# An instruction order that is computed without a port shared by VectorE and GpSimd

## The chip, the core and the metric

The kernel runs on one core of a Trainium2 chip. Five engines of that core work side by side, each with its own queue that it takes in order: PE (TensorE, matmuls), DVE (VectorE), ACT (ScalarE), POOL (GpSimd) and SP (SyncE, which only issues transfers here). They wait for each other through semaphores. The metric is the device time of one execution in microseconds; before the change it was 1264.18 us, the median of three runs (1261.29 to 1264.84).

## The reference

Three layers follow one another: an attention without a square score matrix (softmax of q over the head's width, softmax of k over the sequence, then two products), a two-matrix layer with a quadratic gate, and four experts with ReLU that are weighted by normalised probabilities.

```
q_s = softmax(q, axis=-1);  k_s = softmax(k, axis=2)      # q, k, v: 4 x 8 x 576 x 64
x   = q_s @ (k_s^T @ v)                                   # laid out as 2304 tokens x 512
h   = x @ w_in                                            # w_in 512 x 2048, float64
g   = where(h >= 1, h, where(h <= -1, 0, (h + 1)^2 / 4))
y   = g @ w_out                                           # w_out 2048 x 512, float64
p   = probs / (sum(probs) + 1e-9)
out = sum over e of p[:, e] * (max(y @ w1[e], 0) @ w2[e]) # 4 experts, 512 x 1024 x 512
```

All outputs are float32, and the matmuls keep that precision by splitting each operand into a rounded high part and a low part (the rest).

## The kernel before

**Matmuls in triples.** A product of two operands is three matmuls: low x high, high x low, high x high (lines 912, 913 and 914). One such triple for 512 columns is the unit of PE's work. Most of PE's instructions are these. Each operand has to be split first: a cast to the high part (ACT or DVE, line 387 or 389) and a subtraction that leaves the low part (line 392, on DVE or on POOL; `combine` chooses the engine).

**Tiles and stages.** The 2304 tokens are five blocks (512, 512, 512, 256, 512). Blocks 0 and 1 make the first pass; blocks 2, 4 and 3 the second. In each pass the gated layer comes first ("a"), 16 chunks of 128 of its width, and then the four experts ("b"). For the experts, and in the second pass for the gated layer too, two blocks of tokens are multiplied together by a scheme of Strassen's kind: seven products instead of eight, for which sums and differences of the operands are formed. `prepare` (not quoted) does that for the tokens: T1 to T4 are differences, and seven operands (B11, T2, B21, T3, T1, T4, B22) are split, each in two halves. These steps read two operands from SBUF, and run when a block's last sums arrive, that is at the passage from "a" to "b": at about 240 to 272 us in the first pass and 815 to 850 us in the second.

**The head.** The attention of batches 0 and 1 (eight units of two heads) runs at the start, while the first weights arrive. The weights of the gated layer are float64. DVE and ACT turn each half of a chunk from its two 32-bit words into a high and a low part (`split_double`, lines 623, 627, 629, 631, 635, 642, 646: six instructions on DVE; the low part is done with line 646). The two parts are also written back to memory for the second pass (line 656, `kept`). Attention steps on DVE are the maximum of k (737, 742), of q (831), sums (850), reciprocals (852, 853, 805, 808) and the low part of x (889); POOL subtracts and scales q (line 392 on 640 columns).

**What sets the order.** Nothing is ordered by hand. `Order` holds a set of tasks (Python generators), each of which yields what it wants next: an engine with a duration, a choice of engines, a buffer, or an event. `Order.run` keeps a clock for each engine, takes the instruction that can start first (within 0.05 us the one with the smallest due time), gives it to its engine, and moves the clock. The instructions are issued in the sequence that comes out, so the computed clocks decide two things: the order within each engine's queue, SP's transfers included, and which engine gets a step that may run on either. On the chip, the queues then run as fast as their semaphores let them.

The durations are formulas by width (`dve`, `dve2`, `act`, `pool`, `pe`). DVE's work has two kinds. `dve` is an instruction that reads PSUM or is a reduction; `dve2` is one from SBUF to SBUF with two operands, or a fast copy. The table `HELD` says which clocks an instruction of each kind occupies.

Of the kernel before, what the change touches and what calls it, by code (L numbers as in the profile page):

```python
# [20 lines left out]
PE, ACT, DVE, POOL, SP = "PE", "ACT", "DVE", "POOL", "SP"  # L21


DVE2, PORT = "DVE2", "PORT"
HELD = {PE: (PE,), ACT: (ACT,), DVE: (DVE,), DVE2: (DVE, PORT), POOL: (POOL, PORT), SP: (SP,)}


class Event:
# [36 lines left out]
class Order:  # L65
# [63 lines left out]
    def run(self):  # L129
        while self.tasks:  # L130
            seq = None
            while seq != self.seq:
# [5 lines left out]
            assert ways, "no task can go on"  # L138
            start, e = min((w[0], HELD[w[1]][0]) for w in ways)
            _, start, _, e, d, t = min(  # L140
                (self.rank(w[3], e), w[0], w[3].seq, w[1], w[2], w[3])
                for w in ways if HELD[w[1]][0] == e and w[0] <= start + self.NEAR
            )
            self.now = max(self.now, start)
            for r in HELD[e]:
                self.clock[r] = start + d
            e = HELD[e][0]
            self.load[e] = (start, self.busy(e, start) + d)
# [11 lines left out]
    def way(self, t):  # L160
# [3 lines left out]
        for e, d in [t.want] if isinstance(t.want, tuple) else t.want:  # L164
            own = HELD[e][0]
            start = max(
                t.time - (self.HOP if own == t.engine else 0.0), *(self.clock[r] for r in HELD[e])
            )
# [1202 lines left out]
```

## Time and profile before

| | |
|---|---|
| median of three runs | 1264.18 us |
| the profiled execution | 1265.98 us |
| its span, first to last instruction | 1264.2 us |
| mean granted TensorE clock | 0.986 of full speed |
| PE busy | 1218.1 us (96%) |
| DVE busy | 709.7 us (56%) |
| ACT busy | 521.8 us (41%) |
| POOL busy | 572.4 us (45%) |

Matmuls overlap, so that a single one shows 0.39 us where one follows the other every 0.23 us. An engine's busy time counts the time in which at least one of its instructions runs. A DVE or POOL instruction that is held up after its start shows as a longer one, not as idle time.

### The profile page before, as it was taken

To read this page: it belongs to the slowest core of one execution; us is meant where nothing else is said; L and a number is where in the kernel's file an instruction comes from. 1 tells how busy PE (TensorE), PEld (TensorE's weight loads), DVE (VectorE), ACT (ScalarE), POOL (GpSimd) and SP (SyncE) were. 2 spreads that over 40 slices of the span, in tenths; PEclk is the share of its full clock that TensorE was granted. 3 is DMA by queue.
4 is the path that set the end of the run, shared out by engine and by line. 5 is a ranking of instruction groups with operands and counts; after the bars stand their busy time and mean duration, and the time that the engine had idled before them with its cause. 6 is when DMAs were issued, how large, how long until landed. Compare 5 with 4: busy or idle time off the path is not lost.

```text
span 1264.2 us, 15633 instructions
## 1 busy us (share of the span) xinstructions
PE 1218.1 (96%) x5692; PEld 1002.2 (79%) x5692; DVE 709.7 (56%) x1137; ACT 521.8 (41%) x986; POOL 572.4 (45%) x560
## 2 busy tenths in 40 slices
PE   6789999988999999999999999999999999999998
PEld 4468888767888788888878888878888888888886
DVE  5887989666655655435563555874344334343333
ACT  4477676633433433323565453633223132232320
POOL 2312222666645556543565746656243353432500
PEclk9889999989999999999999999999999999999999
DMA  7665665304323212111422221112111111211003
GB/s 195 169 186 186 199 182 172 111 18 125 96 65 109 76 47 85 34 65 37 135 82 100 84 102 49 51 34 67 34 61 39 34 34 34 67 34 34 17 1 84
DMA packets 86733, 105.39 MB, mean 83 GB/s; under 512 B 29056, under 2 KB 61824, under 8 KB 86656
## 3 DMA queue, kind: packets, MB, share of 16 engines
q1 hardware_dynamic: 86656, 104.40, 26.9%
q8 instruction: 45, 0.74, 0.2%
q14 instruction: 32, 0.26, 0.1%
HBM read 82.87 MB, written 21.50 MB: 83 GB/s over the span
## 4 chain that ended last, share of the span: by engine, by line
PE 84%; DVE 8%; ACT 3%; DMA 2%; issue 1%; SPq 1%; POOL 0%; DVEq 0%; ACTq 0%; POOLq 0%
PE bank L912 27%; PE bank L913 26%; PE bank L914 26%; PE bank L798 2%; PE bank L876 1%; DVE cv L631 1%; DVE cv L635 1%; PE bank L866 1%; DVE x L392 1%; DVE acc L392 1%; DVE cv L1228 1%; DVE cv L642 1%; DVE w L646 1%; DVE acc L1293 1%; DMA acc<-in_v_dram 1%
## 5 line engine op out<-in xcount | busy, mean ns | idle before, releaser
L912 PE MATMUL bank<-x,w 128*128 128x512 f32 (+1 forms) x880 | 329.3, 374 | 8.7 <-DVE w L646 5.4
L913 PE MATMUL bank<-x,w 128*128 128x512 f32 (+1 forms) x880 | 325.2, 370 | 6.2 <-DVE x L392 6.2
L914 PE MATMUL bank<-x,w 128*128 128x512 f32 (+1 forms) x880 | 324.0, 368 | 0.0
L392 POOL TENSOR_TENSOR w<-raw,w 128x512 fp32r<-128x512 f32 (+1 forms) x128 | 159.7, 1253 | 284.0 <-ACT w L387 277.8
L912 PEld LDWEIGHTS bank<-x,w 128*128 128x128 f32 x880 | 167.2, 190 | 43.2 <-DVE w L646 7.0
L913 PEld LDWEIGHTS bank<-x,w 128*128 128x128 f32 x880 | 167.4, 190 | 34.5 <-DVE x L392 8.2
L914 PEld LDWEIGHTS bank<-x,w 128*128 128x128 f32 x880 | 167.2, 190 | 27.5
L1309 DVE SCALAR_TENSOR_TENSOR acc<-bank,pn,acc 128x512 f32<-128x512 f32 x126 | 87.9, 748 | 125.0 <-PE bank L914 125.0
L387 ACT CAST w<-raw 128x512 fp32r<-128x512 f32 (+1 forms) x191 | 109.6, 600 | 73.1 <-PE bank L914 66.0
L912 PE MATMUL bank<-w,gate 128*128 128x512 f32 x342 | 138.7, 406 | 0.5 <-DVE gate L1204 0.5
L392 POOL TENSOR_TENSOR gate<-cv,gate 128x512 fp32r<-128x512 f32 (+1 forms) x54 | 68.6, 1271 | 147.0 <-ACT gate L387 132.0
L913 PE MATMUL bank<-w,gate 128*128 128x512 f32 x342 | 133.9, 392 | 0.0
L914 PE MATMUL bank<-w,gate 128*128 128x512 f32 x342 | 133.9, 392 | 0.0
L392 POOL TENSOR_TENSOR w<-cv,w 128x512 fp32r<-128x512 f32 x80 | 104.7, 1309 | 59.0 <-ACT w L387 48.7
L387 ACT CAST w<-cv 128x512 fp32r<-128x512 f32 x112 | 69.3, 619 | 118.9 <-POOL cv L392 95.1
L1202 ACT ACTIVATE gate<-bank 128x512 fp32r<-128x512 f32 (+1 forms) x73 | 40.5, 555 | 127.5 <-PE bank L914 73.8
L912 PE MATMUL bank<-w,gate_late 128*128 128x512 f32 x234 | 91.1, 390 | 0.0
L913 PE MATMUL bank<-w,gate_late 128*128 128x512 f32 x234 | 91.1, 389 | 0.0
L914 PE MATMUL bank<-w,gate_late 128*128 128x512 f32 x234 | 91.0, 389 | 0.0
L913 PE MATMUL bank<-gate,w 128*128 128x512 f32 (+1 forms) x216 | 81.3, 376 | 1.4 <-POOL gate L392 1.3
L912 PE MATMUL bank<-gate,w 128*128 128x512 f32 (+1 forms) x216 | 81.7, 378 | 0.7 <-ACT gate L387 0.6
L914 PE MATMUL bank<-gate,w 128*128 128x512 f32 (+1 forms) x216 | 81.0, 375 | 0.0
(154 smaller groups left out, 2003.2 us busy)
## 6 DMA issues: line engine op xcount, KB each, us to landing
raw<-in_moe_w_dram SPq DMA_DIRECT2D x64, 512.0 KB, 3.5
kept<-w SPq DMA_DIRECT2D x64, 256.0 KB, 3.8
raw<-kept SPq DMA_DIRECT2D x32, 512.0 KB, 3.3
raw<-in_moe_w_in_dram SPq DMA_DIRECT2D x16, 512.0 KB, 4.3
raw<-in_moe_w_out_dram SPq DMA_DIRECT2D x16, 512.0 KB, 4.2
out_dram<-acc SPq DMA_DIRECT2D x36, 128.0 KB, 2.4
wide<-in_k_dram SPq DMA_DIRECT2D x24, 160.0 KB, 3.1
wide<-in_v_dram SPq DMA_DIRECT2D x48, 80.0 KB, 2.6
```

The source lines that it names most:

```text
L387: nc.scalar.copy(out=dst, in_=src)
L392: (nc.vector if engine == DVE else nc.gpsimd).tensor_tensor(**kw)
L631: nc.vector.scalar_tensor_tensor(out=f, in0=low, scalar=2.0 ** -32, in1=ti, op0=ALU.mult, op1=ALU.add)
L635: nc.vector.scalar_tensor_tensor(out=mi, in0=top, scalar=-0x80000000, in1=mi, op0=ALU.bitwise_and, op1=ALU.bitwise_or)
L642: nc.vector.tensor_scalar(out=ti, in0=mi, scalar1=-0x800000, scalar2=None, op0=ALU.bitwise_and)
L646: nc.vector.scalar_tensor_tensor(out=lo, in0=f, scalar=2.0 ** -20, in1=t, op0=ALU.mult, op1=ALU.mult)
L798: nc.tensor.matmul(bank[:, :N], ek[:, c, :], vt_buf[:, c * N:(c + 1) * N], start=(c == 0), stop=(c == NC - 1),)
L912: nc.tensor.matmul(ps, al, bh, start=first, stop=False, **kw)
L913: nc.tensor.matmul(ps, ah, bl, start=False, stop=False, **kw)
L914: nc.tensor.matmul(ps, ah, bh, start=False, stop=last, **kw)
L1202: nc.scalar.activation(out=gh, in_=h, func=AF.Relu)
L1309: nc.vector.scalar_tensor_tensor(out=dst, in0=p, scalar=by, in1=dst, op0=ALU.mult, op1=ALU.add)
```

## The change

Before, an instruction of the kind `dve2` occupied DVE's clock and a clock named PORT, and a POOL instruction POOL's clock and PORT; so the computed order never lets the two run at the same computed time. Now each occupies its engine alone. Formulas, choices and tasks are unchanged.

```diff
 DVE2, PORT = "DVE2", "PORT"
-HELD = {PE: (PE,), ACT: (ACT,), DVE: (DVE,), DVE2: (DVE, PORT), POOL: (POOL, PORT), SP: (SP,)}
+HELD = {PE: (PE,), ACT: (ACT,), DVE: (DVE,), DVE2: (DVE,), POOL: (POOL,), SP: (SP,)}
```

The order differs on every engine. Three places are shown. In these rows a name is that of the written tile, then those it reads; numbers tell buffers apart (`w` weight parts, `raw` weights as loaded, `cv` temporaries, `x` operands of the matmuls, `acc` and `wide` buffers of attention and of sums).

The first is DVE's queue in the head. Before, from its 33rd instruction on:

```order
L889 TENSOR_TENSOR x_73<-bank_143,x_71 128x256
L642 TENSOR_SCALAR cv_124<-cv_123 128x512
L737 TENSOR_TENSOR wide_153<-wide_151 128x256
L889 TENSOR_TENSOR x_77<-bank_143,x_75 128x64
L889 TENSOR_TENSOR x_73<-bank_143,x_71 128x256
L805 TENSOR_SCALAR rk_168<-bank_142 128x2
L808 RECIPROCAL rk_168<-rk_168 128x2
L737 TENSOR_TENSOR mk_163<-wide_153 128x128
L737 TENSOR_TENSOR mk_163<-mk_163,wide_151 128x128
L646 SCALAR_TENSOR_TENSOR w_93<-cv_125,cv_124 128x512
```

The same place of DVE's queue now, from the 33rd instruction on:

```order
L642 TENSOR_SCALAR cv_124<-cv_123 128x512
L646 SCALAR_TENSOR_TENSOR w_93<-cv_125,cv_124 128x512
L629 TENSOR_SCALAR cv_127<-raw_121 128x512
L631 SCALAR_TENSOR_TENSOR cv_128<-raw_121,cv_127 128x512
L889 TENSOR_TENSOR x_73<-bank_144,x_71 128x256
L635 SCALAR_TENSOR_TENSOR cv_126<-raw_121,cv_126 128x512
L642 TENSOR_SCALAR cv_127<-cv_126 128x512
L646 SCALAR_TENSOR_TENSOR w_95<-cv_128,cv_127 128x512
L623 TENSOR_SCALAR cv_130<-raw_122 128x512
L889 TENSOR_TENSOR x_77<-bank_141,x_75 128x64
```

The first two conversions (w_93, w_95) have moved ahead of the keys of batch 1 (L737 on `wide`), of which there is none here yet; before, w_95 was the 69th instruction, and now it is the 40th.

The second is SP's queue in the head, where the key loads of batch 1 go to `wide`. Before:

```order
L787 DMA acc_88<-in_v_dram 64x5x64 x4
L689 DMA wide_151<-in_k_dram 64x2x320 x2
L478 DMA raw_120<-in_moe_w_out_dram 128x512
L787 DMA acc_90<-in_v_dram 64x5x64 x4
L689 DMA wide_154<-in_q_dram 64x2x320 x2
L689 DMA acc_91<-in_k_dram 64x2x320
L656 DMA kept_0_356<-w_92 128x512
L656 DMA kept_0_356<-w_93 128x512
```

And SP's queue now, from the same transfers on:

```order
L478 DMA raw_120<-in_moe_w_out_dram 128x512
L787 DMA acc_88<-in_v_dram 64x5x64 x3
L656 DMA kept_0_315<-w_92 128x512
L656 DMA kept_0_315<-w_93 128x512
L787 DMA acc_88<-in_v_dram 64x5x64
L787 DMA acc_90<-in_v_dram 64x5x64 x3
L656 DMA kept_1_343<-w_94 128x512
L656 DMA kept_1_343<-w_95 128x512
L787 DMA acc_90<-in_v_dram 64x5x64
L689 DMA wide_152<-in_k_dram 64x2x320 x2
```

The load of k for batch 1 has moved behind the writes of two converted halves, which wait for DVE's line 646.

The third is POOL's queue at the passage to the experts in the second pass (815 to 850 us). Before, from its 412th instruction on:

```order
L392 TENSOR_TENSOR cv_123<-acc_91,acc_89 128x512
L392 TENSOR_TENSOR cv_129<-acc_91,acc_89 128x512
L392 TENSOR_TENSOR w_119<-cv_125,w_115 128x512
L392 TENSOR_TENSOR cv_130<-raw_121 128x256
L392 TENSOR_TENSOR x_76<-acc_90,x_75 128x1024
L392 TENSOR_TENSOR x_86<-cv_123,x_85 128x512
```

The same place of POOL's queue now, from its 417th instruction on; x_82 stands three instructions ahead of these rows:

```order
L392 TENSOR_TENSOR cv_125<-acc_91,acc_89 128x512
L392 TENSOR_TENSOR cv_126<-acc_91,acc_89 128x512
L392 TENSOR_TENSOR x_74<-acc_91,x_73 128x512
L392 TENSOR_TENSOR acc_89<-acc_89 128x512
L392 TENSOR_TENSOR x_84<-acc_91,x_83 128x512
L392 TENSOR_TENSOR w_105<-raw_121,w_104 128x512
L392 TENSOR_TENSOR x_84<-acc_91,x_83 128x512
L392 TENSOR_TENSOR w_107<-raw_121,w_106 128x512
L392 TENSOR_TENSOR x_72<-acc_89,x_71 128x512
L392 TENSOR_TENSOR x_76<-acc_90,x_75 128x1024
```

POOL has taken the operand steps x_74, acc_89, x_84 (two halves) and x_72, with x_82 six in all; before, DVE had them, and both halves of x_86 are now DVE's.

## Rows read from the trace of the kernel before

**Rows 1.** The page's first part: each engine's busy time.

```profile
PE 1218.1 (96%) x5692; PEld 1002.2 (79%) x5692; DVE 709.7 (56%) x1137; ACT 521.8 (41%) x986; POOL 572.4 (45%) x560
```

**Rows 2.** Stages: PE, PEld, DVE, ACT, POOL busy; clock; DMA share; GB/s.

```profile
0.00:12.00 12.00, 4.77 (x9) 2.44 (x9) 3.00 (x9) 5.08 (x22) 2.46 (x17) 1.00 0.77 220
12.00:100.00 88.00, 70.73 (x294) 50.16 (x294) 70.87 (x157) 50.62 (x114) 25.98 (x34) 0.88 0.66 185
100.00:240.00 140.00, 138.83 (x608) 113.31 (x607) 120.72 (x189) 99.18 (x161) 44.81 (x35) 1.00 0.55 175
240.00:272.00 32.00, 24.96 (x90) 18.59 (x89) 23.47 (x27) 11.64 (x20) 17.75 (x13) 0.84 0.08 28
...
815.00:850.00 35.00, 32.25 (x155) 26.30 (x154) 26.60 (x34) 13.23 (x24) 23.38 (x19) 0.95 0.09 30
850.00:1258.00 408.00, 408.00 (x1981) 345.46 (x1980) 162.53 (x251) 107.81 (x197) 150.95 (x143) 1.00 0.13 40
1258.00:1264.20 6.20, 0.72 (x4) 0.26 (x2) 1.43 (x2) 0.00 (x0) 0.00 (x0) 0.85 0.41 94
```

**Rows 3.** PE's waits over the span: us in total, times, longest.

```profile
PE bank L740 <- DVE mk L737: 9.1, 2, 6.0
PE bank L913 <- DVE x L392: 6.2, 4, 3.9
PE bank L912 <- DVE w L646: 5.4, 4, 3.1
```

**Rows 4.** Timeline of DVE and POOL, 203 to 210 us: start, us, instruction.

```profile
203.05 0.43 DVE L642 TENSOR_SCALAR cv<-cv 128x512 int32<-128x512 int32 x1
...
207.70 0.68 DVE L635 SCALAR_TENSOR_TENSOR cv<-raw,cv 128x512 int32<-128x512 int32 x1
207.81 1.73 POOL L392 TENSOR_TENSOR gate<-cv,gate 128x512 fp32r<-128x512 f32 x1 [8.20 <-ACT gate L387]
208.42 1.40 DVE L642 TENSOR_SCALAR cv<-cv 128x512 int32<-128x512 int32 x1
```

**Rows 5.** DVE's groups in 100 to 240 us: busy us, mean ns, idle before.

```profile
L635 DVE SCALAR_TENSOR_TENSOR cv<-raw,cv 128x512 int32<-128x512 int32 x23 | 19.6, 851 | 0.0
...
L1228 DVE TENSOR_TENSOR cv<-bank,cv 128x512 f32<-128x512 f32 x26 | 17.9, 687 | 15.0 <-ACT cv L1220 14.8
...
L642 DVE TENSOR_SCALAR cv<-cv 128x512 int32<-128x512 int32 x23 | 14.7, 639 | 0.8
```

**Rows 6.** Timeline of DVE, SP and PE in the head.

```profile
19.76 1.18 DVE L631 SCALAR_TENSOR_TENSOR cv<-raw,cv 128x512 f32<-128x512 uint32 x1
...
22.55 1.27 SPq L689 DMA_DIRECT2D wide<-in_k_dram  x2
...
88.11 0.78 PE L912 MATMUL bank<-x,w 128*128 128x512 f32 x1 [3.10 <-DVE w L646]
88.68 0.63 PE L913 MATMUL bank<-x,w 128*128 128x512 f32 x1
```

**Rows 7.** Timeline of DVE and PE at the first passage to the experts.

```profile
260.23 3.43 DVE L392 TENSOR_TENSOR acc<-acc 128x512 f32<-128x512 f32 x2
263.58 2.89 DVE L392 TENSOR_TENSOR x<-acc,x 128x512 fp32r<-128x512 f32 x2
265.39 0.80 PE L913 MATMUL bank<-x,w 128*128 128x512 f32 x1 [3.87 <-DVE x L392]
...
269.25 0.39 PE L913 MATMUL bank<-x,w 128*128 128x512 f32 x1
```

**Rows 8.** Timeline of DVE and POOL at the second passage.

```profile
838.97 5.77 DVE L392 TENSOR_TENSOR x<-acc,x 128x512 fp32r<-128x512 f32 x4
840.01 2.49 POOL L392 TENSOR_TENSOR x<-acc,x 128x1024 fp32r<-128x1024 f32 x1 [4.64 <-ACT x L387]
...
845.29 1.27 POOL L392 TENSOR_TENSOR w<-raw,w 128x512 fp32r<-128x512 f32 x1
...
847.05 2.48 DVE L392 TENSOR_TENSOR x<-acc,x 128x512 fp32r<-128x512 f32 x4
```

## The prediction

> **What bounds the kernel now.** I read the page's busy line first, then a table of stages, then what PE waits for, and last the single instructions at which it waits. PE is busy 1218.1 of 1264.2 us [rows 1]. So the order can move only the 46.1 us in which PE is not busy, and the time in which its clock is low. The table of stages puts both in places [rows 2]. PE is not busy for 7.2 us before 12 us, 17.3 in 12 to 100, 1.2 in 100 to 240, 7.0 in 240 to 272, 2.8 in 815 to 850, none in the 408 us up to 1258, and 5.5 in the tail; 5.1 are left for 272 to 815. A mean granted clock below 1.00 is a mixture of the two levels, 2.4 and 1.2 GHz: 0.88 in 12 to 100 is a loss of up to 10.6 us (0.12 x 88), 0.84 in 240 to 272 up to 5.1 us, 0.95 in 815 to 850 up to 1.8 us. The clock is low where PE stood still before: after the wait of 3.87 us that ends at 265.39 the first matmul takes 0.80 us, and at 269.25 one takes 0.39 us again [rows 7].
>
> So three places count: the head (attention of two batches beside the first weights), the passage to the experts at 240 to 272, and the same passage of the second pass at 815 to 850. Of the waits of PE [rows 3], those for VectorE's weights (L646, 5.4 us) belong to the head; those for operands of the experts (L392, 6.2 us) are 3.9 us at 265.39 and 2.3 us in 815 to 850. A fourth place has little idle PE and little room: in 100 to 240 DVE is busy 120.7 of 140 us.
>
> **Does the port exist here?** L642, a TENSOR_SCALAR from SBUF to SBUF, takes 0.43 us at 203.05 and 1.40 us at 208.42, where it starts beside a POOL subtraction that is itself stretched to 1.73 us from 1.27 [rows 4, 8]. So it does. In 100 to 240, L635 and L642 average 851 and 639 ns where undisturbed ones take 680 and 430; L1228, which reads one operand from PSUM, stays at 687 [rows 4, 5]. That is 23 x 0.17 = 3.9 us on L635 and 23 x 0.21 = 4.8 us on L642. If the other four lines of a conversion hold half of the latter each, the stretch holds 3.9 + 4.8 + 9.6 = 18 us of such waiting (an estimate). POOL ran 35 instructions there [rows 2], so each cost DVE about 0.5 us, although this order was computed to keep the two apart. By then the real times have drifted from the computed ones, and the keeping apart fails in nearly half of the cases.
>
> **The change, part by part.** PE's matmuls are the same, with their widths. Between engines little moves: four differences of weights go from POOL to DVE, four of expert operands from DVE to POOL, and four casts from ACT to DVE. What changes is the sequence.
>
> *Head.* DVE now converts w_95 before it starts on the keys of batch 1, where it came some thirty instructions later; by the last attention instruction eight weight halves are converted instead of five, and both orders meet at the ninth (w_109, instruction 163 in both). On PE, 25 triples of FFN matmuls stand ahead of the last attention matmul instead of 12. Gain: the waits for L646 are 5.4 us [rows 3], one of them 3.10 us long with matmuls of 0.63 us behind it [rows 6]; 3.4 us at half the clock are 1.7 us more. Of these 7 us I count 6. Cost: SP's queue is in order, and its key load for batch 1 now stands behind two pairs of writes of converted weights, the second of which needs w_95. DVE reaches its conversion step L631 at 19.76 us [rows 6], and w_95 ends 15 instructions later; at 0.53 us each (between L642 and L635 undisturbed) that is 28 us, and the load goes near 30 us, where it went at 22.55 [rows 6]. Batch 1 is then about 8 us late. The cover is the 13 further triples: 608 matmuls took 138.8 us in 100 to 240 [rows 2], so a triple is 0.68 us and the cover 8.9 us. If it fails (it needs batch 0, whose v loads also move behind the first pair of writes), the 8 us count in full. The conversions also fall beside POOL's attention steps; four collisions more at nearly 1 us, as in rows 4, are 4 us. Net: -6 + 0 + 4 = -2 us, with ends at -17 (all idle PE of 12 to 100) and +12 (8 late, 4 of collisions).
>
> *100 to 240.* The same instructions in nearly the same rows. A collision can cost at most a whole POOL step, 1.27 us [rows 8], instead of 0.5: 35 x 0.77 = 27 us, of which DVE's 19.3 idle us can swallow a part. I take +1, with ends 0 and +8 (27 - 19).
>
> *240 to 272.* On DVE the low half x_72 of one operand now comes before the difference that leads to x_82, where it came behind x_82. PE waits for such a low half until 265.39, and DVE runs four two-input steps there from 260.23 to 266.47 beside POOL, 3.43 and 2.89 us for two each, instead of some 1.3 [rows 4, 7]. One step more ahead is 0.7 to 1.7 us. Against it, no weight step stands on POOL any more between the last two gate steps ahead of the passage. I take +1; ends -3 and +3.
>
> *815 to 850.* POOL now holds five steps of the experts' operands more (x_82, x_74, acc_89, x_84 twice, x_72, less x_86), DVE five fewer. Before, four splits on DVE took 5.77 us beside POOL's 2.49 us, and four took 2.48 us a little later [rows 8]. In the new order POOL has a dozen steps in a row there, so every two-input step of DVE can wait for one. Between the last 512-wide eviction and x_80, which PE needs for its second product, stand five two-input steps, where six did and four 256-wide evictions. Less: one step of 0.7 us and four evictions at half of L1228's 0.69 us, together 2.1 us. More: up to 1 us on each of five, I take 0.8. That is +2; ends -3 (PE's waits here and half of the clock loss) and +6.
>
> *The rest* (272 to 815, the steady experts, the tail) I cost at 0: in 850 to 1258 PE is busy all the time, and DVE and POOL are idle for more than half of it [rows 2], which hides shifts of a microsecond. Without that cover it would be the 5 us of 272 to 815 once more.
>
> Sum: -2 + 1 + 1 + 2 + 0 = +2 us on the profiled execution of 1265.98 us, so 1268. That execution is 1.8 us above the median of the runs, 1264.18; on the median the forecast is 1266 us. A difference under 0.3%, 3.8 us, can't be told from none on this kernel's runs, so the forecast is no measurable change.
>
> The Trainium skill, SBUF — State Buffer, section "Who interferes with whom", speaks against the change: a VectorE instruction with two SBUF inputs and a GpSimd instruction that reads SBUF can't run together, and the one that starts second is blocked for the whole of the other. On single instructions this trace agrees (0.97 us more on L642 at 208.42). By that rule alone each collision would cost up to a full POOL step, +8 in 100 to 240 instead of +1, and the sum would be +9.
>
> **Rivals.** *Slower: the port sets DVE's pace.* With nothing to keep them apart, collisions go to a full POOL step wherever DVE works without pause: +8 in 100 to 240, +3 in 240 to 272, +4 in 815 to 850, and the head loses what it gains. That is +15 at full size, 1279, and 1271 at half of it. It decides from the point where DVE's busy time in 100 to 240 passes some 135 of 140 us, or PE's wait for operands in 815 to 850 passes 5 us. For it: DVE's busy share there of 86%, and 0.5 us already lost on each POOL step. Against it: nearly half of the collisions happen already, and in 100 to 240 DVE's rows hardly move.
>
> *Faster: the planned port held the conversions back in the head.* If the earlier conversions keep PE fed, the waits of 5.4 us and 1.7 us of clock go, and 3 us of the further idle and clock loss in 12 to 100: -10, with +2 elsewhere -8: 1256. For it: DVE was idle 17 of the 88 us [rows 2], and a conversion is six instructions of 0.4 to 0.7 us. Against it: the late load of batch 1.
>
> *The change does nothing.* The order changes on every engine, on DVE from its 17th instruction on, so this is out; what is left of it is that the shifts cancel, my forecast.
>
> **Chances.** Forecast (within 3.8 us of 1264.2) 0.38; the slower rival at whole or half size, 0.37; the faster one, 0.25. The time is that of the likeliest, 1266; its own range is 1261 to 1268. For 8 in 10 I leave out a tenth on each side, the better part of the head's best end (-17) and the slow rival's worst: 1254 to 1279.
>
> **What would show it.** Head right: no PE wait for L646 near 88 us, the key load of batch 1 near 30 us, PE's busy time in 12 to 100 at or above 70.7. Head wrong: PE's waits in attention (L798, L876) grow past 10 us. Port: means of L635 and L642 in 100 to 240 above 851 and 639 ns. 815 to 850: PE waits for L392 of 3 to 6 us instead of 2.3, and a lower clock behind them. I am wrong if PE's busy time outside these places falls, above all in 850 to 1258, or if idle PE comes out below 38 or above 58 us in all.

## The result, and the profile after

The changed kernel takes 1283.93 us (median of four runs, 1281.25 to 1284.20) against 1264.51 us before (1261.29 to 1268.12): a ratio of 1.0148, 95% interval 1.0117 to 1.0179. It is 19 us slower. The forecast was 1266 with a range up to 1279; the slower rival named the cause and stopped at 1279.

The profiled execution took 1283.95 us, span 1282.1 us, mean granted clock 0.979. The page's first part and the table of stages answer to [rows 1] and [rows 2]:

```profile
PE 1221.5 (95%) x5692; PEld 1002.5 (78%) x5692; DVE 723.2 (56%) x1140; ACT 521.8 (41%) x982; POOL 582.3 (45%) x561
```

```profile
12.00:100.00 88.00, 66.96 (x281) 47.51 (x282) 69.92 (x155) 46.80 (x106) 25.99 (x33) 0.84 0.65 174
100.00:240.00 140.00, 137.79 (x599) 111.23 (x597) 116.78 (x184) 97.71 (x160) 44.93 (x34) 1.00 0.57 181
240.00:272.00 32.00, 21.96 (x89) 16.12 (x87) 27.18 (x31) 14.12 (x25) 21.34 (x16) 0.92 0.09 32
272.00:600.00 328.00, 324.60 (x1461) 263.00 (x1462) 175.60 (x284) 117.86 (x234) 175.47 (x182) 0.99 0.25 73
600.00:660.00 60.00, 56.30 (x252) 46.18 (x251) 38.66 (x51) 31.68 (x59) 36.27 (x31) 0.97 0.38 114
...
815.00:850.00 35.00, 31.18 (x148) 26.31 (x147) 19.72 (x27) 12.50 (x24) 25.42 (x22) 0.90 0.14 46
850.00:1258.00 408.00, 404.11 (x1971) 341.93 (x1970) 179.64 (x264) 113.78 (x206) 157.67 (x145) 1.00 0.11 34
```

PE stands still for 60.6 us (1282.1 less 1221.5) instead of 46.1, and its matmuls fill 3.3 us more: more of them run at the lower clock (0.84 instead of 0.88 in 12 to 100, 0.90 instead of 0.95 in 815 to 850). That is the whole difference of the spans, 17.9 us. The idle time grew by 4.0 us up to 100, 1.0 in 100 to 240, 3.0 in 240 to 272, 2.0 in 600 to 660 and 1.1 in 815 to 850, and 3.9 us stand behind 850, where there was none. PE's waits by line, and then the long ones in the timeline (the last figure in brackets is the wait, behind it what ended it):

```profile
PE bank L740 <- DVE mk L737: 10.6, 3, 5.8
PE bank L913 <- DVE x L392: 7.5, 3, 3.6
PE bank L912 <- ACT x L387: 5.2, 1, 5.2
PE bank L912 <- DVE acc L1293: 3.8, 1, 3.8
```

```profile
269.20 0.79 PE L912 MATMUL bank<-x,w 128*128 128x512 f32 x1 [5.16 <-ACT x L387]
273.58 0.79 PE L913 MATMUL bank<-x,w 128*128 128x512 f32 x1 [3.59 <-DVE x L392]
...
620.35 0.50 PE L912 MATMUL bank<-x,w 128*128 128x512 f32 x1 [3.16 <-DVE cv L1154]
...
823.96 0.79 PE L912 MATMUL bank<-gate,w 128*128 128x512 f32 x1 [3.82 <-DVE acc L1293]
```

Two more of 1.95 and 1.94 us for the experts' operands follow at 858 and 861. At 269, 273, 824 and 861 the first matmul behind the wait takes 0.79 or 0.80 us instead of 0.39: the clock is at the lower of its two levels, 1.2 GHz. At 620 the matmuls fall to it 1.3 us later.

What DVE did in those waits is one picture, three times. At the first passage (DVE and POOL, start, duration, instruction; compare [rows 7]):

```profile
262.71 1.78 DVE L392 TENSOR_TENSOR cv<-acc,acc 128x512 f32<-128x512 f32 x1
264.41 1.75 DVE L392 TENSOR_TENSOR x<-acc,x 128x512 fp32r<-128x512 f32 x1
266.08 0.68 DVE L1293 TENSOR_TENSOR acc<-bank,acc 128x512 f32<-128x512 f32 x1
266.69 0.67 DVE L392 TENSOR_TENSOR x<-cv,x 128x512 fp32r<-128x512 f32 x1
267.28 1.21 DVE L392 TENSOR_TENSOR acc<-acc,cv 128x512 f32<-128x512 f32 x1
268.42 3.43 DVE L392 TENSOR_TENSOR acc<-acc 128x512 f32<-128x512 f32 x2
```

```profile
262.20 1.74 POOL L392 TENSOR_TENSOR x<-acc,x 128x512 fp32r<-128x512 f32 x1
263.90 1.71 POOL L392 TENSOR_TENSOR w<-raw,w 128x512 fp32r<-128x512 f32 x1
```

Both engines hold a row of two-input steps from SBUF to SBUF and take turns. A DVE step of 0.69 us becomes 1.75 us, one of POOL's of 1.30 us becomes 1.7 us; the eviction L1293, which reads PSUM, keeps its 0.68, and so does the step at 266.69, which starts as POOL ends one instruction. DVE ran 27 instructions in 240 to 272 before and runs 31 now, POOL 13 and 16; DVE is busy 3.7 us longer there, POOL 3.6.

Stretched steps as such are not new: [rows 7] has four in a row. There are more of them. Two groups of DVE's operand steps (shortest, median and longest in ns), first before, then now:

```profile
L392 DVE TENSOR_TENSOR x<-acc,x x28: 677/684/2871, 239.1 to 848.9; 128x512 fp32r<-128x512 f32 x28
L392 DVE TENSOR_TENSOR acc<-acc x10: 674/856/1759, 254.7 to 838.4; 128x512 f32<-128x512 f32 x10
```

```profile
L392 DVE TENSOR_TENSOR x<-acc,x x24: 676/1220/1785, 245.0 to 866.5; 128x512 fp32r<-128x512 f32 x24
L392 DVE TENSOR_TENSOR acc<-acc x9: 679/1755/1785, 268.4 to 855.7; 128x512 f32<-128x512 f32 x9
```

At 620 PE waits for a sum that reads PSUM (L1154, 0.68 us itself); it stands in DVE's queue behind four operand steps:

```profile
613.97 2.38 DVE L392 TENSOR_TENSOR x<-acc,x 128x512 fp32r<-128x512 f32 x2
616.26 1.76 DVE L392 TENSOR_TENSOR x<-cv,x 128x512 fp32r<-128x512 f32 x1
617.95 1.74 DVE L392 TENSOR_TENSOR x<-acc,x 128x512 fp32r<-128x512 f32 x1
619.62 0.68 DVE L1154 TENSOR_TENSOR cv<-bank,cv 128x512 f32<-128x512 f32 x1
...
819.78 2.73 DVE L1224 SCALAR_TENSOR_TENSOR cv<-cv 128x256 f32<-128x256 f32 x2
```

Four steps at 0.69 us are 2.76 us; here they take 5.88. The 3.1 us between are about PE's wait of 3.16 us. At 824 the same is done by two 256-wide steps, 2.73 us together at 819.78 (last line), ahead of the evictions for which PE waits; one such step takes 0.48 us at 818.93.

### The profile page after: what moved, and what is told of

Its sections match the earlier page's. It is cut to its first block, busy times and chain, and to the rows that moved or that the text cites. A ratio compares the mean times of both kernels' runs of the same rounds, so it can differ in the third digit from the quotient of the medians.

```text
span 1282.1 us, 15623 instructions
## 1 busy us (share of the span) xinstructions
PE 1221.5 (95%) x5692; PEld 1002.5 (78%) x5692; DVE 723.2 (56%) x1140; ACT 521.8 (41%) x982; POOL 582.3 (45%) x561
## 4 chain that ended last, share of the span: by engine, by line
PE 81%; DVE 12%; DMA 2%; ACT 2%; issue 2%; POOL 1%; SPq 1%; DVEq 0%; ACTq 0%; POOLq 0%
PE bank L912 26%; PE bank L913 26%; PE bank L914 25%; DVE x L392 2%; PE bank L798 1%; DVE acc L1293 1%; DVE acc L392 1%; PE bank L876 1%; DVE cv L635 1%; DVE cv L631 1%; PE bank L866 1%; DVE cv L1228 1%; DVE cv L1224 1%; DVE cv L629 1%; DMA wide<-in_k_dram 1%
## 5 line engine op out<-in xcount | busy, mean ns | idle before, releaser
L392 POOL TENSOR_TENSOR w<-raw,w 128x512 fp32r<-128x512 f32 x124 | 154.6, 1250 | 290.0 <-ACT w L387 289.3
L392 POOL TENSOR_TENSOR gate<-cv,gate 128x512 fp32r<-128x512 f32 (+1 forms) x54 | 72.5, 1346 | 154.3 <-ACT gate L387 138.8
L912 PE MATMUL bank<-w,gate 128*128 128x512 f32 x338 | 135.5, 401 | 0.0
L914 PE MATMUL bank<-w,gate 128*128 128x512 f32 x338 | 131.9, 390 | 0.0
L913 PE MATMUL bank<-w,gate 128*128 128x512 f32 x338 | 131.8, 390 | 0.0
L912 PE MATMUL bank<-w,gate_late 128*128 128x512 f32 x238 | 92.9, 390 | 0.5 <-DVE gate_late L1204 0.5
L913 PE MATMUL bank<-w,gate_late 128*128 128x512 f32 x238 | 92.7, 390 | 0.0
L914 PE MATMUL bank<-w,gate_late 128*128 128x512 f32 x238 | 92.6, 389 | 0.0
L912 PE MATMUL bank<-gate,w 128*128 128x512 f32 (+1 forms) x216 | 84.1, 389 | 5.1 <-DVE acc L1293 3.8
L913 PE MATMUL bank<-gate,w 128*128 128x512 f32 (+1 forms) x216 | 84.0, 389 | 3.4 <-POOL gate L392 3.4
L914 PE MATMUL bank<-gate,w 128*128 128x512 f32 (+1 forms) x216 | 83.0, 384 | 0.0
```

Of the source, the lines that this page charges most:

```text
L392: (nc.vector if engine == DVE else nc.gpsimd).tensor_tensor(**kw)
L912: nc.tensor.matmul(ps, al, bh, start=first, stop=False, **kw)
L913: nc.tensor.matmul(ps, ah, bl, start=False, stop=False, **kw)
L914: nc.tensor.matmul(ps, ah, bh, start=False, stop=last, **kw)
```

## The experiments

Theory C: the order is slower because DVE and POOL now meet at the port where PE waits for DVE, and each meeting costs DVE the whole POOL step. Rival S: the sequence itself is worse (late loads, steps in the wrong order, more work on POOL), whatever the steps take. Times are medians; ratios are to the kernel before, run on the same chip beside them (1264.35 or 1264.81 us).

**The same orders without the lock.** POOL's step works on 16 columns, and two memsets of the other columns follow. So POOL stays as busy, but reads SBUF for a moment only; what this leaves out is nearly all of the low parts that POOL computes. One edit, in both orders:

```diff
     def combine(engine, **kw):
-        (nc.vector if engine == DVE else nc.gpsimd).tensor_tensor(**kw)
+        if engine == DVE or kw["op"] == ALU.mult:
+            (nc.vector if engine == DVE else nc.gpsimd).tensor_tensor(**kw)
+            return
+        m = 16 if len(kw["out"].shape) == 2 else 4
+        nc.gpsimd.tensor_tensor(
+            out=kw["out"][..., :m], in0=kw["in0"][..., :m], in1=kw["in1"][..., :m], op=kw["op"]
+        )
+        for _ in range(2):
+            nc.gpsimd.memset(f32(kw["out"])[..., m:], 0.0)
```

> Order of the kernel before. Left out: every addition and subtraction of two tensors on POOL works on 16 columns (4 of each chunk) alone, and two memsets of the remaining columns follow it, so that POOL is busy about as long (some 1.2 us for 512 columns, an estimate from the memsets of 0.20 us for 128 columns) but reads two SBUF operands for a tenth or two of a us only. Theory C (the two engines' collisions at the port cost the time): VectorE's SBUF-to-SBUF steps fall back to their undisturbed 0.4 to 0.7 us, the waits for x at the two passages shrink, 1250 to 1260 us. Rival S (the order itself costs it): within 4 us of before.

> The changed order with the same POOL steps as the run beside it (16 columns and two memsets each). Theory C: the loss of 19 us goes almost wholly, this kernel ends within 4 us of the other one or ahead of it, 1245 to 1260 us, and the waits of 5.2 and 3.6 us at 269 and 274, 3.2 at 620 and 3.8 at 824 us go below 1.5 us each. Rival S: it stays 12 to 19 us behind the other one, with the same waits.

Measured: 1248.97 us with the order of before (0.9884, 0.9868 to 0.9901) and 1252.08 us with the changed order (0.9909, 0.9892 to 0.9927). The first is a microsecond below its range. A POOL step still takes 0.22 us and two memsets of 0.51, some 1.25 us together. DVE at the same operand steps in the changed order, and POOL beside it (line numbers are higher by the added lines; L393 is DVE's two-input step):

```profile
252.84 0.68 DVE L393 TENSOR_TENSOR x<-acc,x 128x512 fp32r<-128x512 f32 x1
253.44 0.71 DVE L393 TENSOR_TENSOR cv<-acc,acc 128x512 f32<-128x512 f32 x1
254.07 0.68 DVE L393 TENSOR_TENSOR x<-acc,x 128x512 fp32r<-128x512 f32 x1
```

```profile
252.16 1.09 POOL L400 MEMSET acc<- 128x496 f32 x2
253.21 0.40 POOL L396 TENSOR_TENSOR x<-acc,x 128x16 fp32r<-128x16 f32 x1
253.55 1.09 POOL L400 MEMSET x<- 128x496 f32 x2
```

So the lock costs the old order 15.4 us (1264.35 less 1248.97) and the new one 31.9 (1283.93 less 1252.08). Of the 19.4 us between the two kernels 16.3 are the lock; 3.1 us are left for the sequence itself. That is less than either interval is wide (some 4 us), but the runs of the two kernels don't overlap (1248.03 to 1250.22 and 1250.42 to 1253.38). The long waits at 273 and 620 are gone; one of 1.96 us is left at the first passage and one of 1.89 us where 3.82 stood at 824, both over the 1.5 us expected. Theory C holds, with a small remainder for S. That the low parts are zeros here does not speed up PE: from 850 us on it made 1981 matmuls in 408.0 busy us with the lock, and makes 1894 in 391.1 without it in the same order, 0.21 us each.

DVE's instructions come in the same sequence with the lock and without it, so they can be compared one by one. Those of its two-input line (392; 393 here) are busy 59.45 us with the lock and 43.62 without it in the old order, and 73.98 and 43.51 in the new one: the lock's part rises from 15.8 to 30.5 us. A meeting does not cost more. Of 64 such steps 19 were longer by over 0.1 us, by 0.84 us on average; of 63 it is 35 now, by 0.88. They lose 9.3 us instead of 6.7 in 240 to 276, 5.9 instead of 1.1 in 600 to 660, and 13.9 instead of 6.5 from 815 on. DVE's other instructions lose less than before, 37.4 us instead of 42.0. So what grew is the number of meetings, in the steps for which PE waits.

**Where.** The port counts only in a part of the order's own time (`self.now`):

```diff
             start = max(
-                t.time - (self.HOP if own == t.engine else 0.0), *(self.clock[r] for r in HELD[e])
+                t.time - (self.HOP if own == t.engine else 0.0),
+                *(self.clock[r] for r in HELD[e] if r != PORT or self.now >= 290.0)
             )
```

The second kernel has `self.now < 290.0`, a third one `self.now >= 110.0`; `HELD` is that of before.

> The port counts in the order only from 290 us of the order's own time on: head, weights and first passage are in the changed order, the rest is ordered with the port. Theory P (each passage and the head pay for themselves): 6 to 9 us slower than before, 1270 to 1274, with the waits at 260 to 275 us as in the changed kernel and none over 1.5 us near 620 or 824. Rival H (the head is what is lost and later places only pass it on): 14 us or more slower. Rival L (only the second pass pays): within 4 us of before.

> The port counts only up to 290 us of the order's own time: head, weights and first passage as before, the rest in an order without the port. Theory P: 8 to 12 us slower than before, 1272 to 1277, with waits of 3 us and more near 620 and 815 to 860 us. Rival H: within 4 us of before. Rival L: 14 us or more slower.

Measured: 1267.57 us without the port up to the first passage (1.0026, 1.0015 to 1.0037) and 1277.95 without it behind that passage (1.0116, 1.0099 to 1.0133): +3.2 and +13.6, together 16.8 of the 19.4 us. The early part came out below its range of 6 to 9, the late part a little above its own. By the times alone rival L is hardly worse: +3.2 lies within its 4 us, and +13.6 just below its 14. But the whole interval of the early part lies above 1, and its waits say where the loss is. Both show the waits of the changed kernel in their places and only there. The late one:

```profile
614.27 0.80 PE L913 MATMUL bank<-x,w 128*128 128x512 f32 x1 [3.15 <-DVE cv L1155]
...
818.78 0.79 PE L913 MATMUL bank<-gate,w 128*128 128x512 f32 x1 [3.82 <-DVE acc L1294]
...
851.49 0.50 PE L914 MATMUL bank<-x,w 128*128 128x512 f32 x1 [1.96 <-DVE x L393]
854.41 0.79 PE L914 MATMUL bank<-x,w 128*128 128x512 f32 x1 [1.96 <-DVE x L393]
```

The early one waits 5.14 us at 266.71 and 3.59 at 271.09, 3.6 us more than the 1.24 and 3.87 us of before; that is all of its loss, so its head costs nothing. That head is the changed kernel's own: in the two traces every engine's instructions come in the same sequence up to 330 us.

> The port is left out of the order only up to 110 us of the order's own time. Forecast's step 'head': -2 us (-17 to +12), so 1260 to 1264 if it held by itself. Theory P (the head is neutral, the loss is at the passages): within 4 us of before. Rival H (the late loads of batch 1 cost): 1268 us or more.

Measured: 1270.50 us (1.0047, 1.0033 to 1.0062), the number of rival H, but not its place. In 12 to 100 us PE is busy 70.31 us (70.73 before); the loss stands in 100 to 240, 132.47 us instead of 138.83. DVE's longest wait for a transfer there ends at 197.57 us:

```profile
197.57 0.23 DVE L426 TENSOR_REDUCE psum_p<-pn 128x18 f32<-128x72 f32 x1 [3.20 <-DMA kept<-w]
...
200.26 0.47 PE L913 MATMUL bank<-gate,w 128*128 128x512 f32 x1 [2.62 <-DVE acc L1294]
```

The normalisation of the probabilities was put where its loads, on SP's queue among the writes of converted weights until 194.5 us, had not come in (the profile names one of the writes as the last release); DVE stood, and PE behind it. The changed kernel does it at 209.7 us without a wait. These 2.6 us are not all: of the 6.4, another 2.9 are three waits of PE for DVE's low half of a weight (L647, at 136.20, 181.01 and 230.70 us). So this kernel says little on the head; that a later place for that step would remove its loss was not tried.

**How long the meeting is.** POOL's additions and subtractions in pieces along the columns, everything else the same (`n` is the number of columns; the third kernel has 128 for 256):

```diff
+        out, in0, in1 = kw["out"], kw["in0"], kw["in1"]
...
+        parts = max(1, n // 256)
+        m = out.shape[1] // parts
+        for i in range(parts):
+            s = slice(i * m, (i + 1) * m)
+            nc.gpsimd.tensor_tensor(out=out[:, s], in0=in0[:, s], in1=in1[:, s], op=kw["op"])
```

> Order of the kernel before; every addition and subtraction on POOL of 512 columns or more is done in pieces of 256 columns (0.76 us each by the profile of before, where 512 take 1.31 us). Theory C (VectorE waits out the whole POOL instruction that it meets): a meeting costs at most 0.76 instead of 1.3 us, so 3 to 8 of the 15 us that the run without the lock gained come back: 1256 to 1261 us, and the four splits of VectorE at the first passage shrink from 1.7 to 1.3 us each. Rival Q (POOL's next piece takes the port again before VectorE does, or the 0.2 us that each step is longer eat it): 1263 to 1268 us.

> The changed order with the same pieces on POOL. Theory C: some half of the 32 us that the lock costs in this order (1284 against 1252) is gone, at least a third: 1266 to 1274 us, and the difference to the run beside it shrinks from 19 to 8 to 14 us. Rival Q: 1282 to 1290 us.

> Order of the kernel before, POOL's additions and subtractions in pieces of 128 columns. Theory C: a meeting now costs VectorE at most some 0.5 us (an estimate: 1.31 us for 512 columns and 0.76 for 256 give 0.49 for 128), so the stretched splits at the first passage take 1.0 instead of 1.2 us, and another 1 to 4 us of the lock's 15 come back: 1257 to 1261. Rival W: each POOL step is 0.6 us longer than undivided, and POOL itself is waited for: 1263 to 1270 us.

Measured: pieces of 256 give 1261.50 us with the order of before (0.9975, 0.9959 to 0.9991) and 1270.25 with the changed one (1.0045, 1.0028 to 1.0062). The 19.4 us shrink to 8.8, and of the 31.9 us of lock in the changed order 13.7 come back, 43%: theory C in its range, in the old order half a microsecond beyond its weak end. The same passage in the changed order, with pieces on POOL (two each):

```profile
260.09 1.01 DVE L393 TENSOR_TENSOR x<-acc,x 128x512 fp32r<-128x512 f32 x1
261.02 0.68 DVE L1304 TENSOR_TENSOR acc<-bank,acc 128x512 f32<-128x512 f32 x1
261.62 0.68 DVE L393 TENSOR_TENSOR x<-cv,x 128x512 fp32r<-128x512 f32 x1
262.22 1.21 DVE L393 TENSOR_TENSOR acc<-acc,cv 128x512 f32<-128x512 f32 x1
263.35 2.35 DVE L393 TENSOR_TENSOR acc<-acc 128x512 f32<-128x512 f32 x2
```

```profile
261.65 2.36 POOL L403 TENSOR_TENSOR w<-raw,w 128x256 fp32r<-128x256 f32 x2
263.98 1.16 POOL L403 TENSOR_TENSOR cv<-raw 128x256 f32<-128x256 f32 x1
```

A stretched DVE step takes 1.2 us where it took 1.75, and 0.68 without the lock: the shorter the POOL instruction that it meets, the shorter it is held, and it gets its turn between the pieces.

Pieces of 128 went the other way, 1271.97 us (1.0059, 1.0039 to 1.0078): rival W, 2 us above its range. DVE's stretched steps at the first passage did fall to 0.94 us, but a piece takes 0.48 us, four of them 1.9 instead of 1.3, and POOL's busy time rises from 572 to 754 us:

```profile
L405 POOL TENSOR_TENSOR w<-raw,w 128x128 fp32r<-128x128 f32 x480 | 212.6, 476 | 216.9 <-ACT w L387 201.4 <-issue 12.3 <-DMA kept<-w 3.0
```

PE then waits for POOL's gates at 247.83 (1.76 us) and 252.80 (2.00). That is not all. The longest wait, 3.66 us at 847.81, is for an operand from DVE, which has no pause from 838.10 on. There one of its steps was held through ten pieces of POOL in a row, until these ended at 842.26:

```profile
838.10 4.72 DVE L393 TENSOR_TENSOR acc<-acc,cv 128x512 f32<-128x512 f32 x1 [0.58 <-POOL cv L405]
```

```profile
837.61 2.14 POOL L405 TENSOR_TENSOR cv<-acc,acc 128x128 f32<-128x128 f32 x5
839.71 1.71 POOL L405 TENSOR_TENSOR w<-cv,w 128x128 fp32r<-128x128 f32 x4
841.39 0.87 POOL L405 TENSOR_TENSOR cv<-raw 128x128 f32<-128x128 f32 x2
```

So DVE does not always get its turn between pieces. Against the same order without the lock, 13 of its instructions are longer here by over 1.3 us, 39.7 us together; with whole POOL steps one is, beside a step of 1024 columns, and with pieces of 256 one, too (2.71 us at 235.59). In all, DVE's instructions lose 57.8 us to whole steps, 41.5 to pieces of 256 and 64.6 to pieces of 128. Rival Q, that POOL's next piece takes the port again before DVE does, failed for 256 columns and holds in part for 128. Why, no run here shows.

**Price or exclusion, and POOL's share.** The first of these keeps the port out of the order and raises the price of POOL's steps; the second takes POOL out of the choice for the operands, the low halves and differences of `prepare` (only its steps are of the class `Soon`):

```diff
 def pool(n):
-    return POOL, 0.18 + n * 0.0022
+    return POOL, 0.18 + n * 0.003
```

```diff
-        t, e = yield pairs([dve2(n), pool(n)])
+        t, e = yield pairs([dve2(n)] if pairs is Soon else [dve2(n), pool(n)])
...
-            t, e = yield Soon([dve2(n), pool(n)])
+            t, e = yield Soon([dve2(n)])
```

> No port in the order, but a POOL step is priced at 1.72 us for 512 columns instead of 1.31, which is what it takes when it alternates with VectorE in the changed kernel. Theory X (what counts is that the order keeps steps apart in time): little is won, 1276 to 1290 us. Rival D (the order only lacks the true durations, and sends too much to POOL): 1264 to 1270 us, near before.

> The changed order's planner, without the choice of POOL for the differences and low halves of the operands at the passages (weights and gates keep it). Theory C: one step on each of two engines that alternate at the port takes 1.74 us, two on VectorE alone 1.38 us, so the waits at 269 and 274 us (8.8 us) fall to 4 to 6 and those at 858 and 861 (3.9) by a third; the 3 us waits near 620 and 824, behind weight steps of POOL, stay: 1277 to 1282 us. Rival M (POOL's operand steps are needed there, VectorE becomes the bound): 1284 us or more.

Measured: 1276.23 us with the dear POOL (1.0092, 1.0068 to 1.0116), at the lower end of theory X. The price wins back 8 of the 19 us; PE still waits 5.30 us at 265, 4.32 at 611 and 4.54 at 816. Here a true duration did not replace the rule that two steps may not overlap. Operands on DVE alone: 1278.49 us (1.0107, 1.0084 to 1.0131), in the range, but only in part for the reason given. The first passage's waits fall from 8.8 to 6.8 us (4 to 6 expected), and the one near 620 to 2.54; but behind the second passage one wait of 4.49 us stands where two gave 3.9.

**Two versions with pieces.**

> The kernel before (port in the order) with pieces of 256 columns on POOL, and the operands' differences and low halves at the passages on VectorE alone. Theory C: at the passages VectorE meets only weight pieces; the waits at 261 and 265 us fall from 5.1 us to 2 to 3, but the order is another one, 1256 to 1262 us. Rival: VectorE alone is too slow for 28 operand steps, 1264 to 1270 us.

> The order of the run beside it, with pieces of 256 columns on POOL. Theory C: 2 to 8 us below the run beside it, as the pieces gave 3 us with the order of before; 1255 to 1262 us. Rival Q: no change.

Measured: 1260.61 us for the kernel before with pieces of 256 and its operands on DVE (0.9973, 0.9958 to 0.9987). At the first passage PE waits 3.0 us instead of 5.1, as expected. In all that is no better than the pieces alone (1261.50); both beat both kernels, by 0.25% the one before and by some 23 us the changed one. The head without the port and pieces: 1266.70 us (1.0015, 1.0002 to 1.0029), 3.8 us below its twin without pieces, as theory C had it, but above its own range, with a wait of 2.87 us at 201 us as in the twin.

## Why the prediction was wrong

The mechanism and two of the three places were in the text, as the first rival; the forecast took the sizes of the other side. By terms, on the profiled execution (the forecast in brackets), PE's idle time grew by 4.0 us up to 100 (-2), 1.0 in 100 to 240 (+1), 3.0 in 240 to 272 (+1), 5.0 from 815 to 1258 (+2) and 2.0 in 600 to 660 (0), and fell by 0.3 in what is left. The 3.3 us more of matmuls, at the lower clock, stood in no term. Together that is 17.9 us; the forecast was +2. Point by point:

- **How many steps meet was mis-sized.** This is the step that failed, in the terms +1 and +2 for the passages and 0 for the rest. I counted one step more at the first passage, five at the second against 2.1 us of gain, and none elsewhere. Measured against the kernels without the lock, 35 of DVE's two-input steps are stretched instead of 19, and lose 30.5 us instead of 15.8. The price that I took at the second passage, 0.8 us, was near (0.84 and 0.88 on average). A full meeting costs 1.75 us less 0.69, that is 1.06, and the first pair in [rows 7] shows it already.
- **The Trainium skill's rule that I set against the sum,** in SBUF — State Buffer, "Who interferes with whom", is that the shared pair of ports is an exclusive lock. These runs agree. They put the price a little under a whole POOL step: beside one that takes 1.30 us alone DVE's is longer by 1.06 us, beside a piece of 0.76 by 0.5, and beside memsets by nothing. I let the rule count for +8 in 100 to 240 only; it decided at the passages. The row that I called its confirmation, L642, reads one operand from SBUF; the steps with two are those of [rows 7].
- **100 to 240: +1 forecast.** PE's busy time fell by 1.04 us (138.83 to 137.79). Right. L635 stayed at 851 ns, L642 fell from 639 to 486; my sign for the port, means above those, did not appear, though the port was the cause. The 18 us of waiting that I estimated here are 13.7 against the order without the lock, and 13.3 in the new order.
- **240 to 272: +1 forecast,** with -3 to +3 as ends. Waits of 8.75 us instead of 5.1: +3.6, and the kernel without the port up to there lost 3.2. Outside.
- **815 to 850: +2 forecast, +6 at most.** Waits of 3.82, 1.95 and 1.94 us instead of 2.8: +5 us, and the clock falls twice. I looked for the loss at x_80, for which PE waits 1.95 us instead of 1.16; most of it came earlier, at an eviction queued behind two stretched 256-wide steps of the gate, which I had not counted.
- **The rest: 0 forecast.** 3.16 us at 620, where the second pass's gated layer gets its operands, a passage of the same kind. I had named the idle half of DVE and POOL in 850 to 1258 as cover; the step at 620 lies outside that stretch and has none. The kernel with the port dropped late has the same wait, 3.15 us.
- **Head: -2 forecast, -17 to +12.** No wait for L646 is left, as said, and the key load of batch 1 goes at 31.62 us (30 said). But the cover failed: PE waits 3.42 us for a v load at 30.64 and 3.17 us for the keys at 46.56, and is busy 3.8 us less in 12 to 100. But the kernels with the port dropped early and in the head alone have the same sequence on every engine up to 130 us at least, and are busy 70.34 and 70.31 us there (70.73 before). So the order's part is near 0.
- **The chances.** 0.37 for slower was too low, and the rival's +15 came near by luck: its largest term, +8 in 100 to 240, measured +1, and neither of its two thresholds was reached (DVE is busy 116.8 us there, not 135, and PE waits 3.9 us for operands behind 815, not over 5). The five operand steps added to POOL could be seen, and what they would meet counted. Two signs of being wrong that I had named did come: 60.6 us of idle PE, over 58, and 404.1 busy us instead of 408.0 in 850 to 1258.

Open: the 3.1 us between the two orders without the lock, and whether every execution of the changed kernel loses the 3.4 us in the head that its trace shows and the other two traces of the same sequence do not.

## What to carry to other kernels

When two engines share a resource, an order must treat the resource as held, not only price the steps: leaving it out cost 19 us here, and a higher price won back 8 of them. Count the meetings at every place where the pacing engine waits for one of the two, not by a mean over a stretch with pauses, and look at every place of the same kind. If the meetings can't be avoided, shorten the instruction that holds, and measure: halves of 256 columns won here, quarters lost, to their own fixed cost and because DVE was passed over by several pieces in a row.

## What the runs showed of the hardware

- POOL memsets of 128x496 beside DVE's two-input steps leave these at 0.68 to 0.71 us: they take no part in the lock, though they write SBUF. A subtraction on POOL, as long as two of them, stretches the same steps to 1.75 us.
- With both queues full of steps of 512 columns the two engines alternate: a DVE step and a POOL step begin about every 1.7 us. One step on each takes 1.7 us, two steps on DVE alone 1.3 us (252.84 to 254.15 in the kernel without the lock). There POOL's help makes the pair slower.
- They do not alternate always: one DVE step was held for 4.72 us through ten POOL pieces of 128 columns.
- POOL's subtraction takes 0.48 us for 128 columns, 0.76 for 256 and 1.31 for 512, on average: some 0.2 us of each are fixed (an estimate from these three).
